# Chunked attention before two MoE layers: rounds of two chunks, reordered loads, and the small part of the first activations on VectorE

## The chip, the core and the metric

The program runs on one core of a Trainium2 chip. The metric is the device time of one execution in microseconds. TensorE (PE in the profile) does the matrix products, its weight loads stand as PEld, VectorE is DVE, ScalarE is ACT, GpSimd is POOL, and SyncE (SP) issues nearly all transfers.

## What is computed

Attention with a decay runs over 2 batches, 8 heads and 768 positions of width 64; then two feed-forward layers follow on its 1536 rows of width 512.

```
for b in range(nb):                                     # blocks of 64 positions
    intra = einsum(qb, kb) * Dmask;  intra = einsum(intra, vb)
    inter = einsum(qb * lam_pow, kv_state)
    out[:, :, sl] = intra + inter
    kv_state = lam_block * kv_state + einsum(kb * rev_pow, vb)
x = attn_out.transpose(0, 2, 1, 3).reshape(B * S, H * D)
h = x @ w_in;  x = elu(h) @ w_out                       # layer 0, d_ff 2048
h = x @ w_in2; out = softplus(h) @ w_out2               # layer 1, d_ff 2048
```

## The kernel before

**Attention.** The kernel takes 12 chunks of 128 positions, six for each batch (CPB = 6). Chunk g is worked off by small steps, and each has a letter: S multiplies q and k (sps), m masks the scores on DVE (sc), X multiplies the scaled q by the state of the chunk before, A multiplies the scores by v, and both add into the two banks xps. T multiplies the faded k by v (stps), t adds this to the faded old state on DVE, f fades the new state on POOL, s scales q on POOL, and k and j scale the heads of k by their decay, the first `k_heads(g)` on ACT and the rest on POOL. h copies xps to xh on ACT and l takes the rest xl on DVE: each number of x is kept as a large part and a small rest, and so is each weight (wh, wl) and each activation g. K turns the first chunk's k, and L issues a list of transfers. Chunk 0 of a batch has no X and its last chunk no T.

The string `ATTENTION` writes all these steps out by hand. Under the manual schedule each engine executes its instructions in the order of the program text, so this string sets the order on every engine. `LOADS` sets the order of the transfers on SP: q is the pair of q and k by columns, k is k and v by rows, and ("w", fc, i) is half i of block fc of the first layer's weights, 512 KB each. Buffers of later weights (wl4, xh2 and others) hold early q, k and v.

On TensorE a product uses a part of the array. S has 64 rows and 128 columns, X has 64 and 64, A and T have 128 and 64, and the feed-forward has 128 and 128. Here a change from one of these shapes to another is called a change of shape.

**Feed-forward.** The work is cut into 96 steps: unit n is one block of 128 columns of d_ff for one tile of 512 rows. `m1(n)` makes the 12 products of x and w_in into a bank hps, `pointwise1` takes it through relu and exp on ACT (v), `pointwise2` combines the two on DVE, copies the large part of g on ACT and subtracts to get its small part; `m2(n)` makes 12 products of g and w_out. `m2` runs LAG = 2 steps behind `m1`. In every step but the last two the small part is made on POOL (L475).

A weight arrives as 8-byte words and is split by `convert` (two ACT instructions, L127 and L128), `shift` (DVE, L132), `high` (ACT, L141, makes wh), `round_up` (DVE, L138) and `rest` (DVE, L144, makes wl). The first four blocks are split by halves in `split_half`, a generator that `half(fc, i, count)` advances by so many stages. The halves (0,0) and (1,0) and the first stages of (2,0) run inside `ATTENTION` (letters c, d, e, g, r) or at the first step; the others run in `early_step(n)` for n = 0 to 4, by the table `HALVES`. Half (3,0) is needed by `m1(3)`, and half (0,1) by `m2(0)`. In `early_step(n)` the text has `m1(n)`, the first stage of the half, `pointwise2(n - 1)`, the other stages, `pointwise1(n)` and `m2(n - LAG)`, in this order.

Of the kernel before, what the change touches and what calls it, by code (L numbers as in the profile page):

```python
# [15 lines left out]
P = 128  # L16
# [27 lines left out]
)  # L44

ATTENTION = """
    S0 m0 K0 k0 S1 m1 s1 A0 h0 T0 j1 k1 t0  # L50
    S2 l0 f0 m2 s2 X1 A1 T1 h1 t1
    S3 k2 l1 f1 m3 j2 X2 s3 A2 T2 h2 t2
    S4 k3 l2 f2 m4 j3 X3 A3 s4 L1 T3 h3 t3
    S5 k4 l3 f3 m5 j4 X4 c0 A4 s5 T4 d0 h4 t4
    S6 g0 l4 S7 e0 m6 X5 j6 k6 A5 m7 s7 A6 h5 l5 T6 h6
    S8 t6 l6 f6 S9 m8 s8 k7 X7 r0 j7 A7 k8 j8 s9 m9 T7 A8 h7 t7 T8 l7 f7
    S10 t8 f8 S11 m10 k9 s10 X8 m11 X9 h8 j9 A9 k10 s11 l8 T9 h9 A10 t9 j10 c1 L2 l9 f9
    T10 t10 X10 d1 h10 A11 g1 l10 X11 e1 h11 r1 l11
"""

STARTS = (
# [3 lines left out]
def body(ctx, tc, consts, attqk, attkv, w1, w2, out):  # L65
# [107 lines left out]
    whalf, spare = {}, {}  # L173

    def load_half(fc, i):
        key, j = ("a", fc) if fc < 2 and i == 0 else ("b", fc) if fc < 2 else ("c", i) if fc == 2 else ("a", i)
        if key not in spare:
            if key == "a":
                spare[key] = acc.tile([P, 2 * DM], U64, tag="yacc0", name="raw0")
            else:  # L180
                spare[key] = stage.tile([P, 2 * DM], U64, tag="raw", name="raw")
        whalf[fc, i] = spare[key][:, DM * j:DM * j + DM]
        nc.sync.dma_start(out=whalf[fc, i], in_=w1[fc][:, DM * i:DM * i + DM])

    def split_half(fc, i):
        r, c = [x[:, :DM] for x in conv_tiles()]
        convert(whalf.pop((fc, i)), r, c)
        yield
        shift(r)
        yield  # L190
        if (fc, 0) not in wh:
            weight_tiles(fc)
        high(r, wh[fc, i])
        yield
        round_up(r, c)
        yield
        rest(c, wh[fc, i], wl[fc, i])

# [40 lines left out]
                in1=qpow[:, :, w - 1:w].to_broadcast([P, NPAIR, w]), op=ALU.mult,  # L239
            )  # L240

    at = {}


    spot = {}
# [22 lines left out]

    def att_load_kv(g):
        home = {2: ("xh2", 0), 3: ("xh2", 1), 4: ("wl4", 0), 5: ("wl5", 0), 6: ("wl6", 0), 7: ("wl7", 0),  # L270
                10: ("wh3", 0), 11: ("wl3", 0)}
        kv = room(*home[g]) if g in home else ap2.tile([P, 2, DM], F32, tag="kv", name="kv")
        o = slice(0 if g else DM, 2 * DM)
        nc.sync.dma_start(out=kv.rearrange("p two n -> p (two n)")[:, o], in_=attkv[g][:, o])
        at[g] += [kv[:, 0], kv[:, 1]]

    def att_prep(g):
        q = at[g][0].rearrange("p (a i) -> p a i", a=NPAIR)
# [10 lines left out]
        turned.append(ps)  # L289

    def k_heads(g):
        return {0: H, 1: 5, 8: 6}.get(g, H // 2)

    def att_prep_k(g):
        k = at[g][2].rearrange("p (h d) -> p h d", h=H)
        y = k if g else turned[0].rearrange("p (h d) -> p h d", h=H)
        for h in range(k_heads(g)):
            A.activation(out=k[:, h], in_=y[:, h], func=AF.Copy, scale=kdecay[:, h:h + 1])

    def att_prep_k2(g):  # L300
        k = at[g][2].rearrange("p (h d) -> p h d", h=H)
        r = slice(k_heads(g), H)
        G.tensor_tensor(
            out=k[:, r], in0=k[:, r], in1=kdecay[:, r].unsqueeze(2).to_broadcast([P, H - k_heads(g), D]), op=ALU.mult)
# [2 lines left out]

    def att_s(g):
        q, k = at[g][:2]
        first = 2 * (g in (1, 7, 8, 11))  # L310
        ps = [ps_y.tile([P, 512], F32, tag=f"y{first + e}", name=f"sps{e}") for e in range(2)]
        for p in range(NPAIR):
            o = slice(P * p, P * p + P)
            for e in range(2):
                r = slice(64 * e, 64 * e + 64)
                T.matmul(ps[e][:, o], k[r, o], q[r, o], start=True, stop=True, skip_group_check=True)  # L316
        sc[g] = ps
# [33 lines left out]
                )  # L351

    def att_intra(g):
        v = at[g][3]
        ps, fresh, last = x_banks(g)
        for p in range(NPAIR):
            o = slice(P * (p // 2), P * (p // 2) + P)
            for c in range(2):
                e = c ^ p & 1
                h = 2 * p + e  # L360
                T.matmul(  # L361
                    ps[e][64 * c:64 * c + 64, o], v[:, D * h:D * h + D], sc[g][:, e, p, :],
                    start=fresh and p < 2, stop=last, skip_group_check=True,
                )
# [99 lines left out]
    def pointwise2(n):  # L464
        ps, v, u = mid.pop(n)
        if u is None:

            V.scalar_tensor_tensor(out=v, in0=v, scalar=-1.0, in1=ps, op0=ALU.add, op1=ALU.max)  # L468
        else:
            V.tensor_tensor(out=v, in0=v, in1=u[0], op=ALU.subtract)  # L470
            V.scalar_tensor_tensor(out=v, in0=ps, scalar=0.0, in1=v, op0=ALU.max, op1=ALU.add)
        g = gp.tile([P, 2, TT], F32R, tag="g", name="g")
        A.activation(out=g[:, 0], in_=v, func=AF.Copy)  # L473
        eng = V if n >= len(order) - LAG else G
        eng.tensor_tensor(out=g[:, 1], in0=v, in1=g[:, 0].bitcast(F32), op=ALU.subtract)  # L475
        gt[n] = g

# [83 lines left out]
    def attention():  # L561
# [66 lines left out]
def _layout(q, k, v, lam, win, wout, win2, wout2):  # L628
# [43 lines left out]
```

## Time and profile before

| | |
|---|---|
| median of 3 runs | 569.91 us (569.04 to 570.88) |
| the profiled execution: its time | 569.41 us |
| its span, first to last instruction | 567.4 us |
| PE busy | 562.6 us (99%) |
| ACT, DVE, POOL busy | 360.4, 341.6, 165.5 us |
| granted TensorE clock, mean | 0.999 |

The time of an execution holds about 2.0 us outside the span. Rows of the timeline give the start in us from the span's first instruction, the length, the engine, the line and the shapes; the bracket is the idle time ahead of it and what ended it. Matmuls overlap, so a PE row's length reaches into the next row, and the time that a block of matmuls takes is read from its start to the next block's start. A matmul of attention stands as two instructions (x16 is 8 in the program). A PE row shows no idle time where the engine waited between two blocks; a wait shows as a longer way from start to start.

### The profile page before, as it was taken

To read this page: it belongs to the slowest core of one execution; us is meant where nothing else is said; L and a number is where in the kernel's file an instruction comes from. 1 tells how busy PE (TensorE), PEld (TensorE's weight loads), DVE (VectorE), ACT (ScalarE), POOL (GpSimd) and SP (SyncE) were. 2 spreads that over 40 slices of the span, in tenths; PEclk is the share of its full clock that TensorE was granted. 3 is DMA by queue.
4 is the path that set the end of the run, shared out by engine and by line. 5 is a ranking of instruction groups with operands and counts; after the bars stand their busy time and mean duration, and the time that the engine had idled before them with its cause. 6 is when DMAs were issued, how large, how long until landed. Compare 5 with 4: busy or idle time off the path is not lost.

```text
span 567.4 us, 7758 instructions
## 1 busy us (share of the span) xinstructions
PE 562.6 (99%) x3023; PEld 467.6 (82%) x3023; DVE 341.6 (60%) x407; ACT 360.4 (64%) x592; POOL 165.5 (29%) x145
## 2 busy tenths in 40 slices
PE   9999999999999999999999999999999999999997
PEld 7988888888888888888888888888888888888886
DVE  6888435545555344013767967666789855656656
ACT  4579656755655654434787876755999756655562
POOL 5662221212212222432531542222122221222210
PEclk9999999999999999999999999999999999999999
DMA  8993112332232121000332200100231000100202
GB/s 331 407 407 122 65 69 97 126 131 94 75 103 120 74 83 66 1 0 1 150 146 77 74 35 40 62 13 2 91 132 74 1 1 1 74 1 0 75 0 75
DMA packets 10692, 49.58 MB, mean 87 GB/s; under 512 B 1184, under 2 KB 1568, under 8 KB 7072
## 3 DMA queue, kind: packets, MB, share of 16 engines
q1 hardware_dynamic: 10368, 48.89, 23.0%
q8 instruction: 23, 0.38, 0.3%
q10 hardware_dynamic: 288, 0.20, 0.2%
q14 instruction: 13, 0.11, 0.1%
HBM read 45.95 MB, written 3.15 MB: 87 GB/s over the span
## 4 chain that ended last, share of the span: by engine, by line
PE 98%; DVE 1%; DMA 0%; issue 0%; DVEq 0%
PE y L506 46%; PE hps L433 15%; PE hps L435 15%; PE hps L434 15%; PE sps L316 2%; PE xps L361 2%; PE xps L348 1%; PE stps L393 1%; DMA const_t<-consts 0%; DVE yacc L553 0%; DVE dmask L227 0%; DVE yacc L508 0%; PE kps L288 0%; DVE yacc L545 0%; DVEq L668 0%
## 5 line engine op out<-in xcount | busy, mean ns | idle before, releaser
L433 PE MATMUL hps<-xh,wh 128*128 128x512 f32 x384 | 149.5, 389 | 0.0
L435 PE MATMUL hps<-xh,wl 128*128 128x512 f32 x384 | 149.5, 389 | 0.0
L434 PE MATMUL hps<-xl,wh 128*128 128x512 f32 x384 | 149.4, 389 | 0.0
L475 POOL TENSOR_TENSOR g<-v,g 128x512 fp32r<-128x512 f32 x48 | 62.9, 1311 | 192.7 <-ACT g L473 192.7
L506 PE MATMUL y<-g,wh 128*128 128x512 f32 x384 | 118.2, 389 | 0.0
L506 PE MATMUL y<-wh,g 128*128 128x512 f32 x382 | 117.7, 389 | 0.0
L475 POOL TENSOR_TENSOR g<-l,g 128x512 fp32r<-128x512 f32 x46 | 60.1, 1306 | 183.6 <-ACT g L473 164.2
L444 ACT ACTIVATE v<-hps 128x512 f32<-128x512 f32 x48 | 28.6, 596 | 98.6 <-PE hps L435 98.4
L468 DVE SCALAR_TENSOR_TENSOR v<-v,hps 128x512 f32<-128x512 f32 x48 | 33.0, 687 | 90.6 <-ACT v L445 90.4
L435 PEld LDWEIGHTS hps<-xh,wl 128*128 128x128 f32 x384 | 72.1, 188 | 15.2 <-DVE wl L144 0.2
L433 PEld LDWEIGHTS hps<-xh,wh 128*128 128x128 f32 x384 | 72.1, 188 | 15.1 <-issue 0.2
L506 PEld LDWEIGHTS y<-g,wh 128*128 128x128 f32 x384 | 72.1, 188 | 14.9
L434 PEld LDWEIGHTS hps<-xl,wh 128*128 128x128 f32 x384 | 72.1, 188 | 14.9
L506 PEld LDWEIGHTS y<-wh,g 128*128 128x128 f32 x382 | 71.7, 188 | 15.3 <-POOL g L475 0.2
L470 DVE TENSOR_TENSOR l<-l,u 128x512 f32<-128x512 f32 x48 | 75.2, 1566 | 4.8 <-DVE u L462 0.5
L462 DVE SCALAR_TENSOR_TENSOR u<-u,e 128x512 f32<-128x512 f32 x48 | 33.6, 700 | 69.4 <-ACT l L456 69.4
L506 PE MATMUL y<-g,wl 128*128 128x512 f32 x192 | 74.7, 389 | 0.0
L506 PE MATMUL y<-wl,g 128*128 128x512 f32 x191 | 74.3, 389 | 0.0
L453 ACT ACTIVATE e<-hps 128x512 f32<-128x512 f32 x48 | 28.6, 597 | 71.0 <-PE hps L435 71.0
L144 DVE TENSOR_TENSOR wl<-c,wh 128x1024 fp32r<-128x1024 f32 (+1 forms) x36 | 49.4, 1372 | 14.6 <-ACT wh L141 13.9
L138 DVE CUSTOM_DVE_ANT_0 c<-r,c 128x2048 uint16<-128x2048 uint16 (+1 forms) x36 | 40.7, 1130 | 4.7 <-ACT c L128 1.8
L506 PEld LDWEIGHTS y<-g,wl 128*128 128x128 f32 x192 | 36.0, 188 | 7.5
(70 smaller groups left out, 604.1 us busy)
## 6 DMA issues: line engine op xcount, KB each, us to landing
raw<-w SPq DMA_DIRECT2D x28, 1024.0 KB, 4.8
early<-attkv SPq DMA_DIRECT2D x8, 512.0 KB, 10.3
raw<-w SPq DMA_DIRECT2D x8, 512.0 KB, 10.2
qk<-attqk SPq DMA_DIRECT2D x6, 512.0 KB, 8.0
early<-attqk SPq DMA_DIRECT2D x6, 512.0 KB, 11.5
out<-yacc SPq DMA_DIRECT2D x7, 256.0 KB, 2.0
kv<-attkv SPq DMA_DIRECT2D x3, 512.0 KB, 10.1
out<-o SPq DMA_DIRECT2D x4, 256.0 KB, 2.3
```

Source lines behind the costliest of these rows:

```text
L138: V.tensor_tensor(out=c, in0=r.bitcast(U32), in1=c, op=ALU.add)
L144: V.tensor_tensor(out=lo, in0=c.bitcast(F32), in1=hi.bitcast(F32), op=ALU.subtract)
L433: T.matmul(ps, wh[fc, 0][:, o], h[:, k, :], start=(k == 0), stop=False)
L434: T.matmul(ps, wh[fc, 0][:, o], l[:, k, :], start=False, stop=False)
L435: T.matmul(ps, wl[fc, 0][:, o], h[:, k, :], start=False, stop=(k == KD - 1))
L444: A.activation(out=v, in_=ps, func=AF.Relu, scale=-1.0)
L453: A.activation(out=e, in_=ps, func=AF.Abs)
L462: V.scalar_tensor_tensor(out=u, in0=u, scalar=-1.0, in1=e, op0=ALU.add, op1=ALU.subtract)
L468: V.scalar_tensor_tensor(out=v, in0=v, scalar=-1.0, in1=ps, op0=ALU.add, op1=ALU.max)
L470: V.tensor_tensor(out=v, in0=v, in1=u[0], op=ALU.subtract)
L475: eng.tensor_tensor(out=g[:, 1], in0=v, in1=g[:, 0].bitcast(F32), op=ALU.subtract)
L506: T.matmul(yps[m], a, b, start=(c == begin and i == 0), stop=(last and i == 2))
```

## The change

The new string puts two chunks together from chunk 2 on (S S, A A, T T, X X where it can). The PSUM banks of S and T, the heads that ACT scales, and the order of the transfers follow it. The rows of k of chunks 5 and 11 are read by no state, since the last chunk of a batch has no T: v of chunk 11 now arrives where k of chunk 5 lay, and one transfer of 512 KB falls away. A new step z (`hold`) writes one element into the buffer of half (2,0) on DVE, so that its transfer and those behind it on SP cannot be issued earlier. In `split_half` `round_up` comes ahead of `high`. In `pointwise2` the small part of g for the five units in `HALVES` is made on DVE.

```
 LOADS = (
-    (("q", 0), ("q", 1), ("k", 0), ("q", 2), ("k", 1), ("q", 3), ("k", 2), ("q", 4), ("k", 3), ("q", 5), ("k", 4),
-     ("w", 0, 0), ("q", 6), ("q", 7), ("k", 5), ("k", 6), ("q", 8)),
...
-    (("w", 3, 0), ("w", 1, 1), ("w", 2, 1), ("w", 3, 1)),
+    (("q", 0), ("q", 1), ("k", 0), ("q", 2), ("k", 1), ("q", 3), ("k", 2), ("q", 4), ("q", 5), ("k", 3), ("k", 4),
+     ("k", 6), ("q", 6), ("q", 7), ("k", 5), ("k", 7)),
+    (("k", 8), ("q", 8), ("q", 9), ("k", 9), ("w", 0, 0), ("q", 10), ("q", 11), ("k", 10), ("w", 1, 0)),
+    (("w", 2, 0), ("w", 0, 1), ("w", 3, 0), ("w", 1, 1), ("w", 2, 1), ("w", 3, 1)),
 )
 ATTENTION = """
-    S0 m0 K0 k0 S1 m1 s1 A0 h0 T0 j1 k1 t0
-    S2 l0 f0 m2 s2 X1 A1 T1 h1 t1
-    S3 k2 l1 f1 m3 j2 X2 s3 A2 T2 h2 t2
-    S4 k3 l2 f2 m4 j3 X3 A3 s4 L1 T3 h3 t3
...
-    T10 t10 X10 d1 h10 A11 g1 l10 X11 e1 h11 r1 l11
+    S0 m0 K0 k0 S1 m1 s1 A0 T0 h0 t0
+    S2 k1 l0 f0 j1 m2 X1 s2 S3 k2 j2 m3 A1 s3 T1 h1 T2 t1 A2 l1 f1 t2
+    X2 X3 h2 L1 S4 l2 S5 m4 j3 k3 A3 m5 j4 k4 f2 A4 s4 T3 h3 T4 t3 l3 f3
+    X4 h4 s5 S6 t4 k6 l4 S7 j6 m6 X5 m7 A5 T6 j7 h5 A6 k7 l5 s7 h6 t6 T7 A7 k8 j8 l6 f6 t7
+    S8 f7 S9 m8 s8 X7 k9 m9 s9 X8 h7 T8 c0 A8 j9 l7 t8 A9 h8 f8 d0 T9 e0 t9
+    S10 l8 S11 m10 z2 s10 k10 X9 m11 f9 X10 h9 j10 A10 g0 l9 s11 T10 h10 r0 A11 c1 L2 t10 l10 X11 d1 h11 e1 g1 l11 r1
 """
...
-        key, j = ("a", fc) if fc < 2 and i == 0 else ("b", fc) if fc < 2 else ("c", i) if fc == 2 else ("a", i)
+        key, j = ("a", fc) if fc < 2 and i == 0 else ("b", fc) if fc < 2 else (("c", fc), i) if fc == 2 else ("a", i)
...
+    def hold(fc):
+        key = spare["c", fc] = stage.tile([P, 2 * DM], U64, tag="raw", name="raw")
+        V.memset(key.bitcast(F32)[:, :1], 0.0)
...
+        round_up(r, c)
+        yield
         high(r, wh[fc, i])
-        yield
-        round_up(r, c)
         yield
         rest(c, wh[fc, i], wl[fc, i])
...
-        return {0: H, 1: 5, 8: 6}.get(g, H // 2)
+        return {0: H, 1: 7, 2: 3, 3: 5, 4: 6, 7: 3, 8: 7, 9: 3, 10: 3}.get(g, H // 2)
...
-        first = 2 * (g in (1, 7, 8, 11))
+        first = 2 * (g in (1, 3, 4, 7, 8, 11))
...
-    spare_y = {1: 3, 2: 2, 3: 3, 4: 2, 6: 0, 7: 2, 8: 3, 9: 0, 10: 1}
+    spare_y = {1: 0, 2: 1, 3: 2, 4: 3, 6: 0, 7: 1, 8: 2, 9: 3, 10: 0}
...
-        eng = V if n >= len(order) - LAG else G
+        eng = V if n in HALVES or n >= len(order) - LAG else G
...
+    k1[CPB - 1] = v1[-1]
...
-        "attkv": np.concatenate([n(k), n(v)], axis=2),
+        "attkv": np.concatenate([k1, v1], axis=2)[:-1],
```

On PE, before the change, from the end of chunk 2's S (the numbers at sps tell the chunks apart) to the start of chunk 3's S there stand X1, A1 and T1:

```order
L316 MATMUL sps_233<-qk 128x128
L348 MATMUL xps<-qk,state 64x128 x8
L361 MATMUL xps<-sc,kv 64x128 x8
L393 MATMUL stps<-kv 64x64 x8
L316 MATMUL sps_281<-early 128x128
```

With the change, from the end of chunk 3's S to the start of chunk 4's S, PE has this (X1 now stands ahead of chunk 3's S):

```order
L320 MATMUL sps_261<-early 128x128
L365 MATMUL xps<-sc,kv 64x128 x8
L396 MATMUL stps<-kv 64x64 x8
L396 MATMUL stps<-early 64x64 x8
L365 MATMUL xps<-sc,early 64x128 x8
L352 MATMUL xps<-qk,state 64x128 x8
L352 MATMUL xps<-early,state 64x128 x8
L320 MATMUL sps_361<-early 128x128
```

A1, T1, T2 and A2, then X2 and X3 now follow each other without another shape between them.

On DVE, at the first two early steps before the change, `pointwise2(0)` and the split of half (0,1) (wl_482), then `pointwise2(1)` and the split of half (3,0) (wl_899):

```order
L468 SCALAR_TENSOR_TENSOR v<-v,hps 128x512
L132 TENSOR_SCALAR r<-r 128x512
L138 ISA c<-r,c 128x1024
L144 TENSOR_TENSOR wl_482<-c,wh_481 128x512
L468 SCALAR_TENSOR_TENSOR v<-v,hps 128x512
L132 TENSOR_SCALAR r<-r 128x512
L138 ISA c<-r,c 128x1024
L144 TENSOR_TENSOR wl_899<-c,wh_898 128x512
```

At the same place with the change (half (0,1) makes wl_686, half (3,0) makes wl_900):

```order
L471 SCALAR_TENSOR_TENSOR v<-v,hps 128x512
L478 TENSOR_TENSOR g<-v,g 128x512
L128 TENSOR_SCALAR r<-r 128x512
L134 ISA c<-r,c 128x1024
L140 TENSOR_TENSOR wl_686<-c,wh_685 128x512
L471 SCALAR_TENSOR_TENSOR v<-v,hps 128x512
L478 TENSOR_TENSOR g<-v,g 128x512
L128 TENSOR_SCALAR r<-r 128x512
L134 ISA c<-r,c 128x1024
L140 TENSOR_TENSOR wl_900<-c,wh_899 128x512
```

The small part of g now stands between v and the shift of the next half; it reads what ACT copies from v (L476).

On ACT, at the end of attention, before the change: the copies h11, the conversion of half (2,0), its high part and the first relu (v<-hps):

```order
L377 ACTIVATE xh_706<-xps 128x2x128 x2
L127 ACTIVATE r<-raw 128x512
L128 ACTIVATE c<-raw 128x512
L141 ACTIVATE wh_840<-r 128x512
L444 ACTIVATE v<-hps 128x512
L445 ACTIVATE v<-v 128x512
L127 ACTIVATE r<-raw 128x512
L128 ACTIVATE c<-raw 128x512
L473 ACTIVATE g<-v 128x512
L141 ACTIVATE wh_481<-r 128x512
L444 ACTIVATE v<-hps 128x512
```

With the change, from the same copies to the first relu:

```order
L381 ACTIVATE xh_669<-xps 128x2x128 x2
L137 ACTIVATE wh_807<-r 128x512
L123 ACTIVATE r<-raw 128x512
L124 ACTIVATE c<-raw 128x512
L137 ACTIVATE wh_841<-r 128x512
L447 ACTIVATE v<-hps 128x512
```

The high part of half (1,0), wh_807, has moved behind h11; from the relu on the order of ACT is as before.

## Rows read from the trace of the kernel before

**Rows 1.** The page's part 4: the chain that ended last, by engine
```profile
PE 98%; DVE 1%; DMA 0%; issue 0%; DVEq 0%
```

**Rows 2.** Busy time by engine, with instructions, of the feed-forward's stretch; then PEclk, DMA
```profile
40.80:563.30 522.50, 522.50 (x2310) 432.43 (x2307) 308.41 (x334) 336.69 (x514) 139.81 (x106) 1.00 0.17 63
```

**Rows 3.** Timeline of PE: round of chunk 2, pairs, end of attention
```profile
9.64 1.16 PE L316 MATMUL sps<-qk 64*128 64x128 f32 x16
10.73 0.67 PE L348 MATMUL xps<-qk,state 64*64 64x128 f32 x16
11.33 1.09 PE L361 MATMUL xps<-sc,kv 128*64 128x128 f32 x16
12.26 0.63 PE L393 MATMUL stps<-kv 128*64 128x64 f32 x16
12.82 1.16 PE L316 MATMUL sps<-early 64*128 64x128 f32 x16
...
32.70 2.07 PE L316 MATMUL sps<-qk 64*128 64x128 f32 x32
34.70 0.67 PE L348 MATMUL xps<-early,state 64*64 64x128 f32 x16
...
35.74 1.09 PE L361 MATMUL xps<-sc,kv 128*64 128x128 f32 x16
36.66 0.64 PE L393 MATMUL stps<-kv 128*64 128x64 f32 x16
37.13 1.06 PE L361 MATMUL xps<-sc,early 128*64 128x128 f32 x16
38.00 0.65 PE L393 MATMUL stps<-early 128*64 128x64 f32 x16
...
40.80 0.50 PE L433 MATMUL hps<-xh,wh 128*128 128x512 f32 x1
```

**Rows 4.** Timeline of DVE: the sum t1 of chunk 1's state
```profile
13.01 0.42 DVE L401 TENSOR_TENSOR state<-stps,faded 128x256 f32<-128x256 f32 x1 [0.89 <-PE stps L393]
```

**Rows 5.** Groups by line and shape: count, busy us, mean ns, idle before
```profile
L279 POOL TENSOR_TENSOR early<-early,qpow 128x512 f32<-128x512 f32 x5 | 6.4, 1280 | 0.0
...
L144 DVE TENSOR_TENSOR wl<-c,wh 128x512 fp32r<-128x512 f32 x8 | 8.9, 1114 | 1.0 <-ACT wh L141 0.5
...
L475 DVE TENSOR_TENSOR g<-l,g 128x512 fp32r<-128x512 f32 x2 | 1.4, 692 | 0.9 <-ACT g L473 0.8
```

**Rows 6.** Timeline of ACT: last copy of attention; early steps 1 and 2
```profile
40.92 0.66 ACT L377 ACTIVATE xh<-xps 128x256 fp32r<-128x256 f32 x2 [0.45 <-PE xps L348]
...
46.17 0.61 ACT L473 ACTIVATE g<-v 128x512 fp32r<-128x512 f32 x1
46.69 0.61 ACT L141 ACTIVATE wh<-r 128x512 fp32r<-128x512 f32 x1
47.21 0.57 ACT L444 ACTIVATE v<-hps 128x512 f32<-128x512 f32 x1
...
49.48 0.62 ACT L473 ACTIVATE g<-v 128x512 fp32r<-128x512 f32 x1
```

**Rows 7.** Timeline of DVE: the split of half (2,0), then early step 1
```profile
42.45 0.42 DVE L132 TENSOR_SCALAR r<-r 128x512 uint32<-128x512 uint32 x1
...
43.80 0.69 DVE L144 TENSOR_TENSOR wl<-c,wh 128x512 fp32r<-128x512 f32 x1
45.16 0.69 DVE L468 SCALAR_TENSOR_TENSOR v<-v,hps 128x512 f32<-128x512 f32 x1 [0.67 <-ACT v L445]
45.77 0.42 DVE L132 TENSOR_SCALAR r<-r 128x512 uint32<-128x512 uint32 x1
```

**Rows 8.** Timeline of PE: start of m2(0), and m1(3)'s first product with wl
```profile
49.11 0.62 PE L506 MATMUL y<-g,wh 128*128 128x512 f32 x2
...
52.28 0.47 PE L435 MATMUL hps<-xh,wl 128*128 128x512 f32 x1
```

**Rows 9.** The page's part 6: weight transfers of 1 MB, us from issue to landing
```profile
raw<-w SPq DMA_DIRECT2D x28, 1024.0 KB, 4.8
```

More of the change, by code (lines that the diff above doesn't have):

```diff
@@ L38 @@
 LOADS = (
[5 rows of a table removed]
[4 rows of a table added]
 )
 ATTENTION = """
-    S0 m0 K0 k0 S1 m1 s1 A0 h0 T0 j1 k1 t0
-    S2 l0 f0 m2 s2 X1 A1 T1 h1 t1
-    S3 k2 l1 f1 m3 j2 X2 s3 A2 T2 h2 t2
-    S4 k3 l2 f2 m4 j3 X3 A3 s4 L1 T3 h3 t3
[L54 to L57, printed above, removed]
-    T10 t10 X10 d1 h10 A11 g1 l10 X11 e1 h11 r1 l11
+    S0 m0 K0 k0 S1 m1 s1 A0 T0 h0 t0
[4 more added lines that the diff above has]
+    S10 l8 S11 m10 z2 s10 k10 X9 m11 f9 X10 h9 j10 A10 g0 l9 s11 T10 h10 r0 A11 c1 L2 t10 l10 X11 d1 h11 e1 g1 l11 r1
 """
@@ L240, in powers @@
             )
-    at = {}
+    at, key, value = {}, {}, {}
     spot = {}
@@ L270, in att_load_kv @@
         home = {2: ("xh2", 0), 3: ("xh2", 1), 4: ("wl4", 0), 5: ("wl5", 0), 6: ("wl6", 0), 7: ("wl7", 0),
-                10: ("wh3", 0), 11: ("wl3", 0)}
+                10: ("wh3", 0)}
         kv = room(*home[g]) if g in home else ap2.tile([P, 2, DM], F32, tag="kv", name="kv")
@@ L274, in att_load_kv @@
         nc.sync.dma_start(out=kv.rearrange("p two n -> p (two n)")[:, o], in_=attkv[g][:, o])
-        at[g] += [kv[:, 0], kv[:, 1]]
+        key[g], value[g] = kv[:, 0], kv[:, 1]
+        if g == CPB - 1:
+            value[NCHUNK - 1] = key.pop(g)
     def att_prep(g):
@@ L291, in k_heads @@
     def k_heads(g):
-        return {0: H, 1: 5, 8: 6}.get(g, H // 2)
+        return {0: H, 1: 7, 2: 3, 3: 5, 4: 6, 7: 3, 8: 7, 9: 3, 10: 3}.get(g, H // 2)
     def att_prep_k(g):
-        k = at[g][2].rearrange("p (h d) -> p h d", h=H)
+        k = key[g].rearrange("p (h d) -> p h d", h=H)
         y = k if g else turned[0].rearrange("p (h d) -> p h d", h=H)
@@ L300, in att_prep_k2 @@
     def att_prep_k2(g):
-        k = at[g][2].rearrange("p (h d) -> p h d", h=H)
+        k = key[g].rearrange("p (h d) -> p h d", h=H)
         r = slice(k_heads(g), H)
@@ L353, in att_intra @@
     def att_intra(g):
-        v = at[g][3]
+        v = value[g]
         ps, fresh, last = x_banks(g)
@@ L381, in att_low @@
             V.tensor_tensor(out=lo, in0=y, in1=hi.bitcast(F32), op=ALU.subtract)
-    spare_y = {1: 3, 2: 2, 3: 3, 4: 2, 6: 0, 7: 2, 8: 3, 9: 0, 10: 1}
+    spare_y = {1: 0, 2: 1, 3: 2, 4: 3, 6: 0, 7: 1, 8: 2, 9: 3, 10: 0}
     def att_state(g):
-        a = at[g]
         ps = ps_y.tile([P, TT], F32, tag=f"y{spare_y[g]}", name="stps") if g else bank("stps")
@@ L392, in att_state @@
                 o = slice(P * p + D * e, P * p + D * e + D)
-                T.matmul(ps[r, D * p:D * p + D], a[2][:, o], a[3][:, o], start=True, stop=True, skip_group_check=True)
+                T.matmul(ps[r, D * p:D * p + D], key[g][:, o], value[g][:, o], start=True, stop=True, skip_group_check=True)
     def att_sum(g):
@@ L567, in attention @@
             h=att_high, k=att_prep_k, s=att_prep, j=att_prep_k2, f=att_fade)
+        ops["z"] = hold
         ops.update({x: lambda fc: half(fc, 0, 1) for x in "cdegr"})
@@ L646, in _layout @@
     pairs = np.repeat(lam.reshape(NPAIR, 2).T, D, axis=0)
+    k1, v1 = n(k), n(v)
+    k1[CPB - 1] = v1[-1]
     return {
```

2 rows, old and new, of the table LOADS are left out of this document.

## The prediction

> **What bounds the kernel now.** I read the chain that ended last first: nearly all of it is PE [rows 1]. So only work that shortens PE's own way, or makes PE wait, can move the time. Then busy time by stretch: from 40.80 to 563.30 us PE is busy throughout, 522.50 us at a granted clock of 1.00 [rows 2]. That is 192 blocks (96 steps, m1 and m2) of 2.72 us each, so this stretch has no room to give, and any wait made in it goes whole into the end. What is left is attention, up to 40.80, and there a PE row hides waits, so I read from start to start. Chunk 2's round takes 1.09 for S, 0.60 for X, 0.93 for A, 0.56 for T, 3.18 in all [rows 3], and the rounds of chunks 3 to 5 repeat this to 0.02 us. An even beat like that is PE's own pace, not that of a DMA or of POOL.
>
> **Attention: what the grouping removes.** A pair S S takes 2.00 [rows 3], against 2 x 1.09: 0.18 saved. A pair X X takes 1.04 against 2 x 0.60: 0.16. A T that is followed by an A takes 0.47 and not 0.56, and an A behind a T 0.87 and not 0.93: 0.15 together. So each change of shape costs PE 0.15 to 0.18 us. Counting from chunk 1's S to chunk 11's X, the old string has 25 changes, the new one 19. Six changes at 0.165 are 1.0 us. The number of matmuls is the same.
>
> Three of the 19 go from X to S, which the old string never does. From below, such a change could be free (then 0.5 more is saved); from above it costs the dearest one seen, 0.18. I take 0.165, since all three kinds seen lie within 0.03 of each other. The Trainium skill says on this, in "TensorEngine Tiling", Key Properties, that a change of tiling mode drains TensorE, whichever modes they are; the trace agrees for the kinds that it has. By that rule the sum stays 1.0, without it it would be 1.5.
>
> **Attention: what the grouping adds.** A round of two asks for the second chunk's inputs sooner. Four places come out late when I set the blocks of the new order after each other.
> X4 stands right behind T4 and needs t3. In the old order a sum ends 1.17 us after its T starts (12.26 to 13.43) [rows 3, 4]; X4's turn comes 0.47 + 0.56 = 1.03 after T3's start, and a hand-over lies between. 0.2 late.
> X8 and X10 need their q scaled by POOL, which takes 1.28 [rows 5] and can start only when that chunk's S has ended. S (1.0 and its drain of about 0.2) and 1.28 are 2.5; the turn comes 2.00 + 0.49. Some 0.1 late at each.
> T7 needs heads of k that ACT scales behind the copy h5: 0.2 by the same reckoning.
> Together 0.6, with bounds of 0 (all covered) and 1.2 (each twice as long). So attention ends 1.0 - 0.6 = 0.4 us earlier, at 40.4, with bounds of 0.2 later and 1.0 earlier (1.5, if X to S is free).
>
> The transfer that falls away gives PE nothing: no PE block of 9.64 to 40.80 is longer than its kind. The held halves start after the second last mask, some 36.4 by the new order; 1 MB from an idle queue lands in 4.8 [rows 9], so 0.5 MB lands by 41.2 at the latest. ACT's turn for half (2,0) comes at 40.4 + 0.12 (h11's start after attention) + 0.66 + 0.52 (h11, and the high part now behind it [rows 6]) = 41.7. Covered by 0.5; if that cover is gone, it delays the loop below by as much as it is late.
>
> **The first feed-forward steps: what moving the small part of g does.** Here I expect the loss. On DVE the shift of the next half now stands behind the small part of g, and that waits for ACT's copy of g. On ACT, the high part of that half waits for the shift, and the next relu stands behind it. So relu, exp, v, g, small part, shift, high, relu becomes one closed loop over ACT and DVE. Before, the small part ran on POOL and the shift followed v directly, at 45.77 [rows 7].
>
> First turn, in the old kernel's times. g ends at 46.17 + 0.61 = 46.78 [rows 6]. The small part on DVE is an operation of 0.69 [rows 5]; to the next start on DVE I take the 0.61 from v to shift [rows 7]. Shift at 47.42 and not 45.77. It lasts 0.42, so high starts at 47.87 and not 46.69, and the relu 0.52 later: 48.39, not 47.21, 1.18 late [rows 6]. wl of half (0,1): from shift to rest 1.35 and 0.69 for rest [rows 7], ending at 49.46. `m2(0)` starts at 49.11 and uses wl as its third product, at 49.56 [rows 8]: just in time.
>
> Second turn. From relu to the next g there were 2.27 us (47.21 to 49.48) [rows 6]; now g is at 50.66 and ends at 51.28, shift at 51.92, high of half (3,0) from 52.37 to 52.99. `m1(3)` would start at 49.11 + 2.72 = 51.83: 1.2 late. Its rest runs from 53.27 to 53.96, and the first product with wl, at 52.28 in the old trace [rows 8], comes at 54.04: 1.75 late, the 1.2 included.
>
> ACT is also later to begin with, since the high part of half (1,0) now follows h11 (0.52 more [rows 6]). Some of that falls into pauses of ACT; between 0 and 0.5 I take 0.2. Loading the late wl costs some 0.05 more, and the old kernel already pays 0.1 there (0.47 and not 0.39 in the row). Net: 1.75 + 0.2 + 0.05 - 0.1 = 1.9 us of waiting on PE, bounds 1.2 (the loop hands over without loss, and DVE gains by the other edits) and 2.5.
>
> From unit 3 on two blocks of PE, 5.44, cover one turn (4.5: 3.34 as before and 1.18), so the rest of the first layer runs without waits. What the move relieves: L144 had a mean of 1.11 with POOL beside it, against 0.69 alone [rows 5, 7]; I have used 0.69 above.
>
> Whether the relu must wait behind high is decided by ACT's order. The row at 40.92 shows ACT idle for 0.45 before the copy h11 [rows 6], with the next conversion, whose data had landed, behind it. The Trainium skill, "Perfetto Trace Analysis", Tensor Engine Instruction, says that ACT, DVE and GpSimd are strict FIFO; the trace agrees. If ACT could pass the relu ahead, the second turn would start 1.18 earlier, and the sum would end near no change, so it is this rule that speaks against the change.
>
> **The sum.** Against the profiled execution: -0.4 + 1.9 = +1.5 us, a span of 568.9 and a time of 570.9. The median of the three runs lies 0.5 above that execution (569.91 against 569.41), so I predict 571.4.
>
> **The rivals.**
> *The move is hidden.* The wait in the second turn doesn't come, because DVE frees itself sooner than I reckon, and only attention changes: -0.4 - 0.1, 569.4. For it: L144's relief. Against it: a turn of 4.5 us meets a PE that gives it 2.72, and the old kernel's `m1(3)` already waited 0.1 for its wl. 17 in 100.
> *Attention at its best as well.* No wait in the rounds and none in the loop: -1.0 - 0.1, 568.8; with X to S free, 568.3. 8 in 100.
> *Slower by more: the held halves are late.* Half (2,0) lands after 41.7 and all that follows on ACT shifts with it. It decides from 0.3 us of lateness (1.7 us in all); for 1 us it gives 572.4. For it: the queue has run empty by then. Against it: the bound of 41.2. With it I count a third turn of the loop that meets `m2(1)`, at a like price. 15 in 100.
> *The clock falls in the new pause.* PE would idle for over 1 us. One block of 2.72 at 1.2 instead of 2.4 GHz costs 2.7 more: 574.1. No row here shows a pause that long inside the kernel. 5 in 100.
> *As forecast* (570.4 to 572.4): 55 in 100.
>
> **How the numbers follow.** 0.3% of the time is 1.7 us, about what a measurement can tell here (the three runs spread over 1.8). Slower by more than that: over 571.6, which is 0.42 of the forecast case (0.23), the held halves and the clock, together 0.43. Faster by more: under 568.2, only the end of the best case, 0.04. Within: 0.53. The range leaves out the best case and the clock: 569.2 to 573.0.
>
> **What would show it.** In the changed trace m1(0) starts near 40.4 (39.8 if the rounds hold no waits); S S and X X take 2.0 and 1.04; X4 starts over 1.05 after T3. The first relu comes 3.1 to 3.5 after m1(0), the second some 4.5 after the first and not 3.34, with ACT idle for about 1 us ahead of the high part; PE's start of m1(3) lies 12.2 to 12.6 after m1(0) and not 11.03, and a second, shorter wait follows at its wl. After that, blocks of 2.72 to the end. I am wrong if the relu's beat stays at 3.3, if m1(0) starts before 39.5 or after 41, or if waits appear after unit 5.

## The result, and the profile after

The changed kernel takes 572.7 us (median of six runs, 572.12 to 573.29), the kernel before 569.64 in the same rounds: a ratio of 1.0052, 95% interval 1.0039 to 1.0064. It is slower by 3.1 us, more than the 1.7 that a measurement can tell here. That lies inside the range of 569.2 to 573.0, but 1.3 us above the predicted 571.4 and 0.3 below the range's end, and only the larger of the two terms of the sum came out as predicted.

The profiled execution has a span of 570.7 us (before 567.4). The page's chain that ended last is PE's again, but less of it (98% in [rows 1]):

```profile
PE 94%; DVE 2%; ACT 1%; issue 1%; DMA 0%; DVEq 0%
```

Busy time by stretch (columns as in [rows 2]; PE's busy time is the second number) shows that feed-forward is no longer one unbroken stretch. It takes 525.21 us, 2.7 more than the 522.50 of [rows 2]; a piece well inside it is full:

```profile
41.59:566.80 525.21, 523.52 (x2311) 432.16 (x2307) 308.82 (x340) 337.50 (x515) 132.91 (x101) 1.00 0.18 65
...
420.00:560.00 140.00, 140.00 (x619) 115.87 (x618) 92.85 (x94) 92.13 (x146) 33.46 (x26) 1.00 0.09 31
```

**The first steps.** ACT's timeline, to be read against [rows 6]: the first relu (L447) at 44.84, the second 4.51 us later and not 3.34. ACT idles 1.10 us ahead of the high part (L137), and the last column says for what: DVE's shift.

```profile
44.84 0.58 ACT L447 ACTIVATE v<-hps 128x512 f32<-128x512 f32 x1
...
47.10 0.61 ACT L476 ACTIVATE g<-v 128x512 fp32r<-128x512 f32 x1
48.81 0.63 ACT L137 ACTIVATE wh<-r 128x512 fp32r<-128x512 f32 x1 [1.10 <-DVE r L128]
49.35 0.58 ACT L447 ACTIVATE v<-hps 128x512 f32<-128x512 f32 x1
...
53.38 0.63 ACT L137 ACTIVATE wh<-r 128x512 fp32r<-128x512 f32 x1 [1.16 <-DVE r L128]
```

DVE's timeline closes the loop (before, in [rows 7], the shift followed v at once): between v (L471) and the shift (L128) stands the small part (L478), and it waits 0.94 us for ACT's copy of g.

```profile
46.12 0.69 DVE L471 SCALAR_TENSOR_TENSOR v<-v,hps 128x512 f32<-128x512 f32 x1 [0.22 <-ACT v L448]
47.74 0.69 DVE L478 TENSOR_TENSOR g<-v,g 128x512 fp32r<-128x512 f32 x1 [0.94 <-ACT g L476]
48.35 0.42 DVE L128 TENSOR_SCALAR r<-r 128x512 uint32<-128x512 uint32 x1
```

PE pays at `m1(3)`, which starts 12.47 us after `m1(0)` (41.59), and again at its first product with wl [rows 8]:

```profile
54.06 0.50 PE L436 MATMUL hps<-xh,wh 128*128 128x512 f32 x1 [1.11 <-ACT wh L137]
54.40 0.39 PE L437 MATMUL hps<-xl,wh 128*128 128x512 f32 x1
54.86 0.50 PE L438 MATMUL hps<-xh,wl 128*128 128x512 f32 x1
```

**Attention.** It ends later, not earlier: `m1(0)` starts at 41.59 (before 40.80 [rows 3]). The next rows are of the timeline of PE and its weight loads (PEld). S4 waits 0.77 for "issue", X4 for the sum t3, X8 and X10 for POOL's scaling, X11 for the sum t10:

```profile
16.64 2.06 PE L320 MATMUL sps<-early 64*128 64x128 f32 x32 [0.77 <-issue]
...
21.75 0.67 PE L352 MATMUL xps<-early,state 64*64 64x128 f32 x16 [0.22 <-DVE state L404]
...
31.48 0.43 PEld L352 LDWEIGHTS xps<-early,state 64*64 64x64 f32 x16 [0.21 <-POOL early L283]
...
37.51 0.43 PEld L352 LDWEIGHTS xps<-qk,state 64*64 64x64 f32 x16 [0.20 <-POOL qk L283]
...
40.99 0.67 PE L352 MATMUL xps<-qk,state 64*64 64x128 f32 x16 [0.45 <-DVE state L404]
```

X11's wait is explained by three rows of the timeline. The sum t10 (L404) stands on DVE behind the rest of half (0,0) (L140), and that rest takes 1.34 us, since POOL's scaling of chunk 11's q (L283) runs beside it:

```profile
38.68 1.28 POOL L283 TENSOR_TENSOR qk<-qk,qpow 128x512 f32<-128x512 f32 x1
...
39.18 1.34 DVE L140 TENSOR_TENSOR wl<-c,wh 128x512 fp32r<-128x512 f32 x1
...
40.44 0.41 DVE L404 TENSOR_TENSOR state<-stps,faded 128x256 f32<-128x256 f32 x1
```

**A wait 360 us later,** in layer 1, where nothing was changed. PE waits for POOL's small part, which takes 1.83 us where its neighbours take 1.30; the DVE operation that began with it takes its usual 0.69:

```profile
409.04 1.30 POOL L478 TENSOR_TENSOR g<-l,g 128x512 fp32r<-128x512 f32 x1 [4.14 <-ACT g L476]
415.42 0.69 DVE L473 TENSOR_TENSOR l<-l,u 128x512 f32<-128x512 f32 x1
415.42 1.83 POOL L478 TENSOR_TENSOR g<-l,g 128x512 fp32r<-128x512 f32 x1 [5.08 <-ACT g L476]
417.31 0.50 PE L509 MATMUL y<-wh,g 128*128 128x512 f32 x1 [0.51 <-POOL g L478]
```

**Where the 3.3 us of span are.** A PE row hides waits, so I measure from matmul to matmul. From S1 to `m1(0)`: 35.08 us against 33.74, 1.34 more. From `m1(0)` to the last matmul: 525.17 against 522.51, 2.66 more, of which the first steps have 1.81 (starts that are later than the usual 0.227 add up to 1.94, before to 0.13) and the late wait 0.79. Against that stands 0.55 that has nothing to do with the change: S0 took 1.09 us in this profile and 1.76 in that of before. Over all thirteen profiles below it took 1.09 to 2.01, whatever the kernel. The two are not independent: `m1(0)` itself starts 0.79 later than before, and in the four profiles with this order of attention (after, e1, e4, e8) it starts at 41.54 to 41.76, though S1 starts anywhere from 6.47 to 7.41. So an early opening is largely waited off behind S1, and part of the 1.34 is its price.

### The profile page after: what moved, and what is told of

Its sections match the earlier page's. It is cut to its first block, busy times and chain, and to the rows that moved or that the text cites. A ratio compares the mean times of both kernels' runs of the same rounds, so it can differ in the third digit from the quotient of the medians.

```text
span 570.7 us, 7751 instructions
## 1 busy us (share of the span) xinstructions
PE 562.8 (99%) x3023; PEld 466.5 (82%) x3023; DVE 341.6 (60%) x413; ACT 361.3 (63%) x594; POOL 158.1 (28%) x140
## 4 chain that ended last, share of the span: by engine, by line
PE 94%; DVE 2%; ACT 1%; issue 1%; DMA 0%; DVEq 0%
PE y L509 45%; PE hps L438 15%; PE hps L437 15%; PE hps L436 15%; PE sps L320 2%; PE xps L365 2%; PE xps L352 1%; PE stps L396 1%; DMA const_t<-consts 0%; DVE xl L385 0%; ACT wh L137 0%; DVE wl L140 0%; DVE sc L332 0%; DVE yacc L556 0%; DVE g L478 0%
## 5 line engine op out<-in xcount | busy, mean ns | idle before, releaser
L478 POOL TENSOR_TENSOR g<-l,g 128x512 fp32r<-128x512 f32 x46 | 60.4, 1314 | 184.0 <-ACT g L476 168.8
L478 POOL TENSOR_TENSOR g<-v,g 128x512 fp32r<-128x512 f32 x43 | 55.6, 1294 | 201.2 <-ACT g L476 201.2
L447 ACT ACTIVATE v<-hps 128x512 f32<-128x512 f32 x48 | 28.6, 597 | 95.3 <-PE hps L438 95.2
L471 DVE SCALAR_TENSOR_TENSOR v<-v,hps 128x512 f32<-128x512 f32 x48 | 32.9, 686 | 90.7 <-ACT v L448 90.6
L140 DVE TENSOR_TENSOR wl<-c,wh 128x1024 fp32r<-128x1024 f32 (+1 forms) x36 | 47.0, 1305 | 15.1 <-ACT wh L137 14.5
```

Source lines behind the costliest of these rows:

```text
L140: V.tensor_tensor(out=lo, in0=c.bitcast(F32), in1=hi.bitcast(F32), op=ALU.subtract)
L447: A.activation(out=v, in_=ps, func=AF.Relu, scale=-1.0)
```

## The experiments

Each profile is cut at the same places: the start of S1, of `m1(0)`, and of the last matmul (us). Times are medians; the kernel before had 569.57 to 569.80 in these rounds.

| kernel | time | ratio to before, 95% | S1 | S1 to m1(0) | m1(0) to the last |
|---|---|---|---|---|---|
| before | 569.64 | | 7.06 | 33.74 | 522.51 |
| after | 572.70 | 1.0039 to 1.0064 | 6.51 | 35.08 | 525.17 |
| e1 small part on POOL | 570.12 | 0.9996 to 1.0013 | 6.54 | 35.10 | 522.62 |
| e2 before, small part on DVE | 571.42 | 1.0019 to 1.0041 | 6.44 | 34.08 | 524.97 |
| e3 t10 first | 572.02 | 1.0027 to 1.0054 | 7.05 | 34.17 | 524.87 |
| e4 nine writes on POOL | 571.70 | 1.0021 to 1.0048 | 7.41 | 34.35 | 524.37 |
| e5 two edits | 569.86 | 0.9997 to 1.0015 | 6.51 | 34.05 | 523.13 |
| e6 ten tiny matmuls | 570.37 | 1.0008 to 1.0026 | 6.59 | 34.61 | 523.16 |
| e7 short queue | 570.08 | 0.9999 to 1.0017 | 6.92 | 34.89 | 523.15 |
| e8 small part behind rest | 570.16 | 1.0000 to 1.0019 | 6.47 | 35.07 | 523.18 |
| e9 three edits | 569.33 | 0.9988 to 1.0006 | 7.20 | 33.88 | 522.54 |
| e10 no second batch's loads | 570.25 | 1.0002 to 1.0023 | 6.80 | 34.11 | 523.10 |
| e11 k of chunk 7 first | 569.82 | 0.9994 to 1.0013 | 7.34 | 33.92 | 522.56 |

### The loop: e1, e2, e8

Theory: the loop of the prediction. Rivals: the held halves, or the high part behind h11, or simply too much work on DVE. e1 takes the move back in the changed kernel, e2 makes it alone in the kernel before.

```
-        eng = V if n in HALVES or n >= len(order) - LAG else G    # e1; e2 adds it to before
+        eng = V if n >= len(order) - LAG else G
```

> The changed kernel with the small part of g of the first five units back on POOL, all else as changed. Loop theory (relu, exp, v, g, small part, shift, high, relu closed over ACT and DVE): the second relu comes about 3.3 us after the first and not 4.5, ACT no longer idles 1.1 us ahead of the high part, PE's waits at m2(0) and m1(3) shrink from 1.94 us in all to about 0.1, and the time falls by 1.8 us, from 572.7 to about 570.9. Rival (the waits come from the high part of half (1,0) standing behind h11, or from the held halves, not from the move): the waits stay and the time stays at 572.7. The late wait of PE for POOL at 417 us (0.8 us) may go as well, since POOL gets five instructions more ahead of it; then 570.1.

> The kernel before with this one edit: the small part of g of the first five units on DVE. Loop theory: attention as before (m1(0) at 40.8), the second relu 4.5 us after the first, m1(3) some 12.3 us after m1(0) and not 11.03, and the time up by 1.2 to 2.5 us, 1.8 the likeliest: 571.4. Rival (the loop needs the changed order of the halves as well): a beat of 3.3 us and 569.6.

e1: 570.12, 2.6 us less; the two relus lie 3.32 apart, and from `m1(0)` on 522.62 us remain, as before. The wait at 417 us went too, as the second number of the expectation had it. e2: 571.42, the predicted figure, with the whole pattern in a kernel whose attention is the old one. (The exact fit is partly luck: from `m1(0)` on its profile has 2.46 us more than before, 1.70 of the loop and 0.76 of the late wait, which the expectation did not count, and `m1(0)` starts 0.28 earlier.) ACT's and PE's timeline, in before's line numbers: the idle 1.09, the relus 4.53 apart, `m1(3)` 12.3 us after `m1(0)` (40.52).

```profile
43.58 0.60 ACT L444 ACTIVATE v<-hps 128x512 f32<-128x512 f32 x1 [0.28 <-PE hps L435]
...
47.57 0.63 ACT L141 ACTIVATE wh<-r 128x512 fp32r<-128x512 f32 x1 [1.09 <-DVE r L132]
48.11 0.58 ACT L444 ACTIVATE v<-hps 128x512 f32<-128x512 f32 x1
...
52.83 0.50 PE L433 MATMUL hps<-xh,wh 128*128 128x512 f32 x1 [1.11 <-ACT wh L141]
```

So the move alone makes the loss; neither the held halves nor the order of their steps is needed for it. e8 asks whether DVE has too much work or only the wrong order. The small part stays on DVE, behind the rest of the half:

```
-        if n - 1 in mid:
-            pointwise2(n - 1)
+        small = pointwise2(n - 1) if n - 1 in mid else None
         half(*first, 4)
+        if small:
+            small()                # V.tensor_tensor(out=g[:, 1], ...)
```

> The changed kernel with the small part of g of the first five units still on DVE, but behind the rest of the half that follows it and not ahead of its shift. Loop theory, by place in the order: the shift no longer waits for ACT's copy of g, the relu's beat falls from 4.5 to about 3.3 us, the waits at m2(0) and m1(3) (1.94 us) shrink to 0.2 or less, and the time falls by 1.8 us to 570.9; the late wait at 417 us (0.8 us) stays, since POOL's instructions are those of the changed kernel. Rival (DVE has too much work with the small part on it, wherever it stands): the beat stays over 4 us and the time at 572 or more.

It takes 570.16, 2.5 us less than the changed kernel (1.8 expected; its span is 2.0 less, with the late wait still in it). DVE's timeline: the shift follows v at once, the small part comes last (L479 here) and waits for nothing.

```profile
46.07 0.69 DVE L471 SCALAR_TENSOR_TENSOR v<-v,hps 128x512 f32<-128x512 f32 x1 [0.22 <-ACT v L448]
46.67 0.42 DVE L128 TENSOR_SCALAR r<-r 128x512 uint32<-128x512 uint32 x1
...
48.24 0.69 DVE L140 TENSOR_TENSOR wl<-c,wh 128x512 fp32r<-128x512 f32 x1 [0.32 <-ACT wh L137]
48.85 0.68 DVE L479 TENSOR_TENSOR g<-v,g 128x512 fp32r<-128x512 f32 x1
```

`m1(3)` starts at 52.56, 11.02 after `m1(0)`, with no wait there. The work on DVE is the same as in the changed kernel; the place in the order was the whole loss.

### X11's wait, and what it is worth: e3, e5, e9

```
-... T10 h10 r0 A11 c1 L2 t10 l10 X11 ...
+... T10 h10 A11 c1 L2 t10 r0 l10 X11 ...        # e3
+... T10 h10 A11 c1 L2 t10 l10 r0 X11 ...        # e5, e9
```

> The changed kernel with the last sum of the state (t10) ahead of the rest of half (0,0) on DVE. If X11 waits 0.52 us because t10 stands behind that rest, A11 to X11 falls from 1.49 us to about 0.97, m1(0) starts 0.5 us earlier after the last S, and the time falls to 572.2. Rival (the rest, now later, makes its wl late for the third product of m1(0), 0.45 us after its start): the wait moves into m1(0) and the time stays at 572.7.

572.02, 0.2 under the expected 572.2. A11 to X11 falls to 0.975, and the rest, now behind POOL's scaling, takes 0.68. DVE's timeline:

```profile
39.71 0.42 DVE L404 TENSOR_TENSOR state<-stps,faded 128x256 f32<-128x256 f32 x1 [0.54 <-PE stps L396]
40.05 0.68 DVE L140 TENSOR_TENSOR wl<-c,wh 128x512 fp32r<-128x512 f32 x1
40.65 0.75 DVE L385 TENSOR_TENSOR xl<-xps,xh 128x256 fp32r<-128x256 f32 x2
```

But of the 0.52 not all arrives: X11 to `m1(0)` takes 0.82 and not 0.60, and `m2(0)` is 0.3 longer. By the order `m1(0)` now waits for the low part l10, which frees its bank; e5, which puts l10 ahead as well and takes e1's edit along, has 0.60 there.

> The changed kernel with the small part of g back on POOL and, on DVE, the sum t10 and the low part l10 ahead of the rest of half (0,0). If both edits act as in the runs that made one of them, the closed loop (1.9 us) and the late wait at 417 us (0.8 us) are gone and A11 to X11 falls from 1.49 to 0.98 us: 570.1 less 0.5 gives 569.6, about the kernel before. Rival (the rest, now last, makes wl late in m1(0)): X11's gain comes back as a wait in m1(0), 570.1.

569.86, a little over the expected 569.6. `m1(0)` starts 1.08 us earlier than in e1 (0.51 of it by X11, the rest because S10 did not stall, below), but from there on e5 has 0.51 more, all of it ahead of `m1(3)`'s first product with wl. Neither theory had that. The rest that makes this wl runs beside POOL's small part and takes 1.55 us (timeline of the three engines):

```profile
50.59 1.47 POOL L478 TENSOR_TENSOR g<-v,g 128x512 fp32r<-128x512 f32 x1 [2.00 <-ACT g L476]
...
51.06 1.55 DVE L140 TENSOR_TENSOR wl<-c,wh 128x512 fp32r<-128x512 f32 x1 [0.16 <-ACT wh L137]
...
52.66 0.50 PE L438 MATMUL hps<-xh,wl 128*128 128x512 f32 x1 [0.46 <-DVE wl L140]
```

In e1 this rest takes as long (1.54), and PE waits only 0.13 for it. What e5 adds is that the 0.51 which X11 gained is PE's alone: ACT and DVE come 0.58 earlier than in e1, so the first relu stands 3.75 us behind `m1(0)` and not 3.25 (3.74 in e6 and e7 too, whose PE waits 0.58 and 0.54 there). So there was something for the small part to relieve, once X11's wait is gone: in e9, where this rest has no POOL beside it, the relu is as late and PE does not wait. The rest takes 0.68 or 0.69 us alone, 1.34 and 1.55 beside POOL. The Trainium skill, "SBUF — State Buffer", section "SBUF: two separate sides", says that DVE (in an operation with two inputs in SBUF) and GpSimd hold a shared pair of ports as an exclusive lock, and that the other one blocks. The rows agree: both slow rests began while POOL's operation ran, and end 0.55 us after it.

e9 joins what helped: e8's order, e5's order of the sums, and e4's writes.

> That kernel with the two other edits that took a wait away: t10 and l10 ahead of the rest of half (0,0), and nine tiny writes on POOL behind attention. The wait of m1(3) for its wl in the kernel of the two edits (0.62 us, where that rest took 1.55 us beside POOL's small part and 0.69 alone) should go too, since POOL has no small part there: 569.86 less 0.6 gives 569.2, 0.4 below the kernel before. Rival (something else on DVE or ACT is late for m1(3)): 569.8, no better than before.

569.33, a ratio of 0.9997 (0.9988 to 1.0006): the wait of `m1(3)` is gone (522.54 from `m1(0)` on), as expected, but the 0.3 us under the kernel before cannot be told from nothing. It is the best version found, and no proof that the grouping pays.

### The late wait: e4

```
             ops[name[0]](int(name[1:]))
+        for _ in range(9):
+            G.memset(qpow[:, :, :1], 0.0)
```

> The changed kernel with nine tiny writes more on POOL right after attention, where it is idle; it then has as many instructions as in the kernel before. If PE's late wait for POOL at 417 us (0.8 us with what follows) comes from a place in POOL's instruction stream (a transfer of the instruction queue starts at 416.09 in the changed kernel, and at 385.60 in the kernel before, where PE does not wait), the wait is gone or elsewhere, the transfer comes some 30 us earlier, and the time falls to about 571.9. Rival (the wait comes from the work that meets in that step): it stays at 417 us and the time at 572.7.

571.7, 1.0 less, and no late wait. POOL's timeline: the step at 415 us now takes 1.34.

```profile
387.44 1.29 POOL L478 TENSOR_TENSOR g<-l,g 128x512 fp32r<-128x512 f32 x1 [4.15 <-issue]
...
415.28 1.34 POOL L478 TENSOR_TENSOR g<-l,g 128x512 fp32r<-128x512 f32 x1 [4.78 <-ACT g L476]
```

The trace records transfers of instructions too, on two queues, one with 16 KB a transfer (PE's, below) and one with 8 KB. A transfer of the second moved from 416.09 to 388.42 us. Over the kernels the two go together: PE waits where that transfer starts at 414.08 (e8, 0.79 again), 415.03 (e2), 416.09 (after) and 416.19 us (e3, only 0.2). In before, e1, e4, e5, e6, e7, e9 and e11 it starts at 385.6 to 388.4, in e10 at 402.65, and PE does not wait. So the wait depends on the place in POOL's instruction stream, and moving five operations from POOL to DVE changed that place. In the step in question POOL begins 0.42 us after ACT's copy of g has ended (415.00) and not 0.13, as at 412.46 in before; DVE's next operation then gets in first. It is POOL's 198th record in all four kernels that wait; in the others the last small part ahead of the transfer is the 196th, and it begins 0.13 after the copy. The transfer itself starts 0.7 to 0.9 us after the late operation has begun, so it marks the place and is not what POOL waits for; what costs those 0.3 us was not tried. A long small part alone costs nothing: every profile has one of 1.8 us between 314 and 317 us, begun on time, and PE does not wait there.

### S4's wait for "issue": e6, e7, e10, e11

No semaphore ends S4's wait. Its first weight load, the one that waits for a semaphore, ran at 15.80 (timeline of PEld); the matmul behind it, with no semaphore of its own, came 0.84 us later, at 16.64:

```profile
15.80 0.18 PEld L320 LDWEIGHTS sps<-early 64*128 64x128 f32 x1 [0.17 <-issue]
```

PE's transfers of instructions are 16 KB each, and PE's records, counted in order from the first, show stalls of 0.15 us and more that no row explains at the 450th, the 962nd and the 1218th only, which lie 256 or 512 apart (each 256th record from the 450th on is called a place below). The nine largest, and the kernel before:

```
kernel  transfer starts  PE's record  PE goes on  difference  stall
after   14.18             450th       16.64       2.46        0.84  (S4)
e2      14.05             450th       16.50       2.45        0.23
e3      14.12             450th       16.57       2.45        0.29  (S4)
e4      14.35             450th       16.83       2.48        0.18  (S4)
e9      14.09             450th       16.65       2.57        0.22  (S4)
e11     14.48             450th       17.01       2.53        0.44  (S4)
e6      26.34             962nd       28.94       2.60        0.56  (S8)
e1      33.03            1218th       35.56       2.53        0.56  (S10)
e7      33.69            1218th       36.24       2.55        0.34  (S10)
before  14.20 to 32.74    450th to 1218th         2.57 to 2.87  none
```

Where PE stood, it went on 2.45 to 2.60 us after the start of a transfer; where it hardly stood or not at all, the least was 2.32 (e5) and 2.41 (e2). The old order uses 256 instructions in two rounds of 3.18, that is 6.36 us, and the transfers come every 6.0 to 6.7 us (before, after, e1): in the kernel before, PE was 0.1 to 0.4 us from standing at each of the four places. The new order sends T T, A and X X through one behind the other just ahead of the 450th, the last 128 of these instructions in 2.5 us.

e6 moves the place by twenty instructions:

```
         for i in range(count):
             T.matmul(ps, zero[:, :P], zero, start=True, stop=True)
+        for i in range(10):
+            T.matmul(ps[:32, :32], zero[:, :32], zero[:, :32], start=True, stop=True)
```

> The kernel of the two edits with ten matmuls of 32 columns more behind the warming ones, in the pause ahead of S0: twenty PE instructions more, nothing else. Supply theory: PE's instructions come in blocks of 256; the first stall seen falls ahead of PE's 450th instruction (loads of weights and matmuls counted), which is the first of S4 in the changed kernel, and it ends 2.46 us after a transfer of the instruction queue starts. Then the place moves back by twenty instructions, into X3, S4 follows X3 without a wait of its own, and the 128 instructions ahead of the place take 2.34 us and not 2.62, so the stall in the rounds grows by some 0.3 us: up to 569.9. Rival (S4 waits for its data or its bank): the wait stays at the first matmul of S4, and the time is that of the two edits.

570.37, half a microsecond over e5. The expected stall in X3 did not come, since the transfer started at 12.19, earlier than in any other kernel. A stall came two blocks further on, inside S8, where no kernel without the ten matmuls had one, and at PE's 962nd record: 

```profile
28.17 0.48 PE L322 MATMUL sps<-early 64*128 64x128 f32 x2
28.94 1.04 PE L322 MATMUL sps<-early 64*128 64x128 f32 x13 [0.29 <-issue]
```

It starts two matmuls into S8, at a weight load that waits for no semaphore. So S4's wait is for instructions, not for q or a bank. The profiles of e1 and e8, whose attention is the changed kernel's to the letter, say the same: S3 waits for q there (0.27 and 0.66), the transfer starts at 13.49 and 13.41, S4 follows X3 without a wait, and PE stands in S10 instead (0.56 and 0.17). What makes the transfers late? e7 keeps the loads' queue short, e10 leaves out the loads of chunks 6 to 11.

```
-    (("q", 0), ("q", 1), ... ("k", 5), ("k", 7)), (("k", 8), ... ("w", 1, 0)),      # e7
+    (("q", 0), ... ("q", 4)), (("q", 5),), ..., (("k", 3),), (("k", 4),), (("k", 6),), ...
+    # each called where DVE should free it, behind a V.memset of its first column

     def att_load(g):                                                               # e10
+        if g >= CPB:
+            at[g] = at[{8: 2, 9: 5}.get(g, g % 2)]
+            return
```

> The kernel of the two edits with the transfers of chunk 5's q and later issued one at a time, each behind a one-column write on DVE, three to five transfers ahead of its landing and not eight; order and sizes are the same. Supply theory with a queue: the transfers of the instruction queue now wait 3 to 4 us behind the loads that were issued ahead of them (before: PE reaches an instruction 256 further on 6.1 to 6.5 us after the last place, as fast as they come). With a shorter queue they come 1 to 2 us sooner, no stall is left at S4 or S10, and the time falls by up to 0.8 us, to about 569.0. Rival (the instruction queue has its turn whatever else is queued): the transfers start as far behind PE as now, the stalls stay, and the time is 569.6, or more if a load comes late.

> The kernel of the two edits without the transfers of q, k and v for the second half of the chunks: chunks 6 to 11 work on tiles of the first six, so the output is not the reference's. From about 20 us on nothing but a few weights is in flight. If the transfers of the instruction queue are slow because loads are in flight, they start about 1.1 us after PE has reached the last place (as at 35.46 us in the changed kernel, where the queue had run empty) and not 3.1 to 4.6, and no stall is left from the third transfer on. Rival (they start at a fixed distance in PE's own stream): still over 3 us.

e7: the transfers start 3.8 to 4.1 us after PE has reached the last place, as in e5 (3.7 to 3.8): the rival is right, and the depth of the loads' queue (three to six loads in flight here, up to eight in e5) doesn't matter. Loads that came late cost it 0.7 us on the way to S7. e10: without loads in flight the third transfer starts 1.0 us after the place, the next two 0.65 and 0.3 ahead of theirs, and PE uses them 5.5 us and more after their starts. So loads in flight make the instructions late, however few are queued. e10's time says little, as e5, its base, had lost only 0.05 there.

e11 takes away one more of the late places, T7's, on top of e9:

```
-... T6 j7 h5 A6 k7 l5 s7 h6 ...
+... T6 j7 k7 h5 A6 l5 s7 h6 ...
```

> The kernel of three edits with ACT's heads of k of chunk 7 ahead of the copy h5 and not behind it. If T7 waits 0.23 us for these heads, its block (0.69 us to the next) falls to 0.46, m1(0) starts 0.2 us earlier, and the time falls from 569.3 to 569.1, 0.5 below the kernel before. Rival (T7 waits for POOL's heads, or the gain is waited off for the instruction queue in the round behind it): T7 stays at 0.69 or a wait of 0.2 us comes in S10, and the time stays at 569.3.

T7's block falls from 0.69 to 0.465, as the theory had it, and the time does not fall: 569.82. In its profile S4 stalls 0.44 (0.22 in e9), so S1 to `m1(0)` is the same, 33.92. But S4 stands ahead of T7, where the edit changes nothing: from T7 on the way to `m1(0)` is 13.70 us and was 13.88 in e9. So the gain is there in the profile, and the medians, whose intervals overlap, can't tell whether the time keeps it.

## Why the prediction was right in time, and where it was wrong

**The loop: right, in place and size.** Predicted 1.9 us, measured 1.81; the second relu 4.5 after the first, 4.51; `m1(3)` 12.2 to 12.6 after `m1(0)`, 12.47; e2, e1 and e8 show that the move alone makes it, and by its place.

**Six fewer changes of shape: right, but not in the time.** S S and X X take 1.99 and 1.05; a change from X to S costs what others do (X4 takes 0.60 ahead of S6 as X5 does ahead of A5, and S6 S7 take 1.99 as S10 S11 do behind a T), so 1.0 us is saved and not 1.5.

**"Four places come out late": right in kind, short in size and in number.** X4 0.30 (0.2 predicted), T7 0.23 (0.2), X8 and X10 0.19 and 0.17 (0.1 each; POOL's scaling starts 1.28 us after that chunk's S and not 1.2): 0.89 and not 0.6. A fifth was missed, X11, 0.52: I set PE's blocks after each other and looked only at the producer, not at what DVE has ahead of t10, and took that rest at its time without POOL beside it.

**"An even beat like that is PE's own pace, not that of a DMA or of POOL": the step that failed.** The beat was PE's, but the instructions come by DMA at the same beat. Where a group of blocks goes faster, PE waits for them: 0.84 us at S4. That, X11 and the 0.29 by which the four places were dearer turn -0.4 into +1.25; 0.05 more is S3 waiting for q, and +1.34 was measured. How much of the 0.84 belongs to the order is open: where S1 starts at 7.05 to 7.41 (e3, e4, e9, e11; 7.06 in before), S4 stands for 0.18 to 0.44 only, so some 0.5 of it may be the price of this profile's early opening, and X11 is then the larger miss. With X11's wait gone and little stall (e9) the new rounds take 33.88 us, and the old ones 33.74: the 1.0 us is paid back whole.

**"The rest of the first layer runs without waits": right; of the second layer I said blocks of 2.72 to the end, and that was wrong** by 0.8 us. I counted what the moved operations do on DVE, and not that POOL's later instructions move up.

**Covered as said:** the held half (2,0) landed at 40.28 and was converted at 42.77 (L123); no load is waited for in the first steps. The dropped transfer gave PE nothing that shows. The granted clock stayed at 1.00 through the pause ahead of `m1(3)`.

By what the prediction itself named, `m1(0)` after 41 and a wait after unit 5 both speak against it. From S1 on the sum was too low by 1.74 in attention, and by `m1(0)` itself, where the better opening of this one profile is counted in, by 1.19 (0.79 later, not 0.4 earlier); it was too low by 0.79 in layer 1. The loop, right to 0.1, carried the time into the range, and that the misses left it there, 0.3 below the end, is luck. None of the rivals describes what happened.

## What to carry to other kernels

When an operation is moved between engines, write down the loop that its queue closes: if a producer on engine A now waits for B, and B's next work waits for A, the beat is the sum of both, and putting the moved operation last in its step can cost nothing where putting it first costs everything. An even beat is no proof of what sets it: two suppliers can run at the same pace, and the margin of the second is measured where the first is made faster. In a kernel that has no wait left, a microsecond can come and go by where an engine's instruction stream is cut, so try a change of a few empty instructions before a story is built on a late wait.

## What was not expected of the hardware

- PE's instructions come during the run, 16 KB for 256 records, and can be used 2.45 to 2.6 us after such a transfer starts (nine stalls). With loads in flight a transfer starts 3.1 to 4.6 us after PE reached the last place, with up to eight loads in flight or with three to six; without loads from 0.65 us ahead of it to 1.2 us behind it.
- At one place in POOL's stream a small part began 0.3 us late and, beside DVE, took 0.5 us longer; nine one-column writes 370 us earlier took that away.
- S0's pace at the start of the kernel differs from profile to profile (1.09 to 2.01 us for the same sixteen matmuls), and a good opening was mostly waited off again, at S3 for q (up to 0.66) or at S4, S8 or S10 for instructions (up to 0.84); of the new orders that opened by 6.6 us only e5 lost less than half a microsecond of it. Why the pace differs was not looked into.
